# Linear attention with decay feeding a routed expert layer: attention with transposed output, alternating halves of the matmul array and interleaved sequences

## The chip, the cores and the metric

The kernel runs on one core of one Trainium2 chip. The metric is the device time of one execution in microseconds. The engines named below are TensorE (PE for its matmuls, PEld for its weight loads), VectorE (DVE), ScalarE (ACT), GpSimd (POOL) and the queue of SyncE (SP), which here only issues transfers.

## What is computed

There are 4 sequences of 768 tokens and 8 heads of 64. Attention is linear with a decay per head, and each token's result (512 numbers) then goes through one of 8 experts.

```python
# attention, per head, with lam the decay
intra = (q_b @ k_b.T) * Dmask @ v_b          # Dmask[i, j] = lam ** (i - j) where i >= j
inter = (q_b * lam_pow) @ kv_state
out_b = intra + inter
kv_state = lam_block * kv_state + (k_b * rev_pow).T @ v_b
# expert layer, x = attention's output as (B, S, 512)
logits = x @ w_gate                           # 8 experts
local_gate = sigmoid(x @ w_local)
e = argmax(logits) if s == 0 or local_gate < 0.5 else previous token's e
out = softmax(logits)[e] * (relu(x @ w1[e]) @ w2[e])
```

All inputs and matmuls are float32.

## The kernel before

There are three stages. **Attention** (function `attention(b)`, L135 to L207) goes through the sequences one after the other and through each in 6 chunks of 128 positions (the reference's blocks of 64 give the same result with chunks of any size). **Routing** (L213 to L347) finds each token's expert and sorts tokens into 31 tiles of 128 slots. **Experts** (L349 to L409) gather each tile's rows from DRAM, run the two matrices of its expert and scatter the result.

Attention loads three chunks at a time, with four transfers on SP's queue (`qt`, `kt`: q and k with the head dimension on the partitions, two heads in the two halves of the 128 partitions; `kn`, `vn`: k and v with positions on the partitions). The experts' first weights (four transfers of 2 MB, L150 and L151) follow the loads of the second half of sequence 0. Then, for each chunk:

- the scores (L168), 8 matmuls: keys as the stationary operand, queries moving, each on 64 rows of the array (one head); the half `u` = 0 first, then `u` = 1. VectorE multiplies each half by the decay mask into `sm` (L170);
- the output `po` (L174, L178): the decayed queries `qd` times the state `kv` (4 matmuls, two heads at once), and for each of 8 heads `sm` as the stationary operand of 128 columns, `v` moving with 64 columns. The positions are on the partitions of the result;
- the state (L184 to L194): 4 matmuls into `pk`; GpSimd scales the old state (L190), VectorE adds `pk` (L192), in two halves;
- the way out: ScalarE copies `po` to `xn` (L196) and issues its transfer to `x_dram` (L197); TensorE transposes `xn` (L200, 4 transposes); ScalarE copies them to `xt` (L202); 4 matmuls with `xt` stationary and the gate's 9 columns moving give the logits in `pl` (L204), which VectorE copies to `lt` once per three chunks (L207).

GpSimd also makes `qd` (L153, three chunks at once) and `kd`, the decayed keys (L156, one per chunk). The order of the instructions on each engine is that of a scheduler, which fills TensorE's waits of one chunk with work of the next. Matmuls in float32 appear in the trace as two records each.

Of the kernel before, what the change touches and what calls it, by code (L numbers as in the profile page):

```python
# [8 lines left out]
F32 = mybir.dt.float32  # L9
I32 = mybir.dt.int32  # L10
U32 = mybir.dt.uint32
# [3 lines left out]
SP = mybir.EngineType.SP  # L15
PSUM = bass.MemoryType.PSUM
# [11 lines left out]
HC = 3                  # chunks per load  # L28
# [9 lines left out]
def kernel(  # L38
    ctx: ExitStack,
    tc: tile.TileContext,  # L40
    qT: bass.AP,
    kT: bass.AP,
    k: bass.AP,
    v: bass.AP,
# [26 lines left out]
    lamb = const.tile([P, H], F32, name="lamb")  # L71
    nc.sync.dma_start(out=lamb, in_=lam.unsqueeze(0).broadcast_to([P, H]))
    wgt = const.tile([P, DT, E + 1], F32, name="wgt")
    nc.sync.dma_start(out=wgt, in_=wg)
# [19 lines left out]
    token = iota("token", [[P, NT]], 1, 1)      # the token's row, plus one  # L94
    whole = iota("whole", [[P, NT]], 0, 0)      # 0, 128, 256, ...

    x_ctx = ExitStack()
    load = x_ctx.enter_context(tc.tile_pool(name="load", bufs=2))
# [4 lines left out]
    # mask[j, u, a, i] = lam[2a + u] ** (i - j) where i >= j, else 0  # L103
# [4 lines left out]
    with tc.tile_pool(name="build", bufs=1) as build:  # L108
# [9 lines left out]
        # lamq[(u d), a, i] = lam[2a + u] ** (i + 1)  # L118
# [16 lines left out]
    def attention(b):  # L135
        kv = att.tile([P, A, 2, DH], F32, name="kv")
        nc.gpsimd.memset(kv, 0.0)
        for half in range(NC // HC):
            r = slice(HC * P * half, HC * P * half + HC * P)
            qt = load.tile([P, A, HC, P], F32, name="qt")  # L140
            nc.sync.dma_start(out=qt.rearrange("p a c i -> p a (c i)"), in_=qT[b, :, :, r])
            kt = load.tile([P, A, HC, P], F32, name="kt")
            nc.sync.dma_start(out=kt.rearrange("p a c i -> p a (c i)"), in_=kT[b, :, :, r])
            kn = load.tile([P, HC, DM], F32, name="kn")
            nc.sync.dma_start(out=kn, in_=k[b, r].rearrange("(c p) d -> p c d", p=P))
            vn = load.tile([P, HC, DM], F32, name="vn")
            nc.sync.dma_start(out=vn, in_=v[b, r].rearrange("(c p) d -> p c d", p=P))
            if b == 0 and half == 1:
                for i in range(2):
                    nc.sync.dma_start(out=w1t[i], in_=w1_src(0))  # L150
                    nc.sync.dma_start(out=w2t[i], in_=w2_src(0))  # L151
            qd = att.tile([P, A, HC, P], F32, name="qd")
            nc.gpsimd.tensor_tensor(qd, qt, lamq.unsqueeze(2).broadcast_to([P, A, HC, P]), ALU.mult)  # L153
            kd = att.tile([P, HC, DM], F32, name="kd")
            for c in range(HC):
                nc.gpsimd.tensor_tensor(kd[:, c].rearrange("p (h d) -> p h d", d=DH),  # L156
                                        kn[:, c].rearrange("p (h d) -> p h d", d=DH),
                                        rev.unsqueeze(2).broadcast_to([P, H, DH]), ALU.mult)
            pl = pa.tile([P, HC, E + 1], F32, name="pl")
            for c in range(HC):  # L160
                ch = HC * half + c
                t = NC * b + ch
                sm = att.tile([P, 2, A, P], F32, name="sm")
                for u in range(2):
                    rows = slice(DH * u, DH * u + DH)
                    ps = pa.tile([P, A, P], F32, name="ps", bufs=2)
# [3 lines left out]
                    nc.vector.tensor_tensor(sm[:, u], ps, mask[:, u], ALU.mult)  # L170
                po = pa.tile([P, A, 2, DH], F32, name="po", bufs=2)
                for a in range(A):
                    if ch:
                        nc.tensor.matmul(po[:, a], lhsT=qd[:, a, c], rhs=kv[:, a],  # L174
                                         start=True, stop=False, skip_group_check=True)
                    for u in range(2):
# [3 lines left out]
                if ch + 1 < NC:  # L180
                    pk = pa.tile([P, A, 2, DH], F32, name="pk")
                    for a in range(A):
                        cols = slice(P * a, P * a + P)
                        nc.tensor.matmul(pk[:, a], lhsT=kd[:, c, cols], rhs=vn[:, c, cols],  # L184
                                         start=True, stop=True)
                    for u in range(2):
                        rows = slice(DH * u, DH * u + DH)
                        d = kv[rows, :, u]
                        if ch:
                            nc.gpsimd.tensor_tensor(d, d, lamq[rows, :, P - 1:P].broadcast_to([DH, A, DH]),  # L190
                                                    ALU.mult)
                            nc.vector.tensor_tensor(d, pk[rows, :, u], d, ALU.add)  # L192
                        else:
                            nc.vector.tensor_copy(d, pk[rows, :, u])  # L194
                xn = att.tile([P, DM], F32, name="xn", bufs=3)
                nc.scalar.copy(xn, po.rearrange("p a u d -> p (a u d)"))  # L196
                nc.scalar.dma_start(out=x_dram[P * t:P * t + P, :], in_=xn)  # L197
                pt = pa.tile([P, DT, P], F32, name="pt")
                for d in range(DT):
                    nc.tensor.transpose(pt[:, d], xn[:, P * d:P * d + P], ident)  # L200
                xt = att.tile([P, DT, P], F32, name="xt")
                nc.scalar.copy(xt, pt)  # L202
                for d in range(DT):
                    nc.tensor.matmul(pl[:, c], lhsT=xt[:, d], rhs=wgt[:, d],  # L204
                                     start=(d == 0), stop=(d == DT - 1))
            t = NC * b + HC * half
            nc.vector.tensor_copy(lt[:, t:t + HC], pl)  # L207

    for b in range(B):
        attention(b)  # L210
    x_ctx.close()

# [1 line left out]
    gidx = route.tile([P, G], U32, name="gidx")     # row of x for each slot  # L214
    sidx = route.tile([P, G], U32, name="sidx")     # row of out for each slot
    gate = route.tile([P, G], F32, name="gate")
    owner = route.tile([1, G], I32, name="owner")   # each tile's expert
    with tc.tile_pool(name="rt", bufs=1) as rt, tc.tile_pool(name="pr", bufs=1, space=PSUM) as pr:
# [4 lines left out]
        # the first of the greatest, as 8 - e  # L223
# [33 lines left out]
        # is[p, e, t]: token (t, p) goes to expert e  # L257
# [4 lines left out]
        # the chosen expert's probability  # L262
# [83 lines left out]
        nc.vector.tensor_tensor(src, src, none, ALU.add)  # L346
        nc.vector.tensor_copy(sidx, src)  # L347

# [97 lines left out]
```

## Time and profile before

| | us |
|---|---|
| two runs | 720.13 and 730.7, median 725.41 |
| span of the profiled execution | 743.7 |
| attention: first scores to the last copy into `lt` | 8.9 to 248.6 |
| experts: first expert matmul to the end | 287.4 to 743.7 |

TensorE is busy 702.7 us of the span (94%), VectorE 128.5 (17%), ScalarE 66.8 (9%), GpSimd 136.3 (18%). The page is one profiled execution. Its second part cuts the span in 40 slices of 18.6 us; PEclk is the clock that TensorE was granted, in tenths of full speed (9 and more is 2.4 GHz throughout, 5 is 1.2 GHz). A timeline row merges neighbouring instructions of the same line and says when the first began, how long they lasted and how many there were.

### The profile page before, as it was taken

What the parts mean: (1) busy time and instruction counts of PE and PEld (TensorE: products, weight loads), DVE (VectorE), ACT (ScalarE), POOL (GpSimd) and SP (SyncE); (2) the same over time, 40 slices, a digit from 0 to 9 for tenths busy, and PEclk for the clock granted to TensorE, in tenths of its full rate; (3) what the DMA queues carried; (4) which work ended last, traced back from release to release, by engine and by line L of the source; (5) the groups of instructions that cost most, each with busy time, mean ns of one, the idle gap of its engine ahead of it and who ended that gap; (6) DMA issues with size and microseconds to landing.
All of it is one profiled execution on the core that took longest, in us unless ns stands there. A gap on an engine that the chain in (4) does not pass through costs nothing. (4 is left out here: it accounts for less than half of the span.)

```text
span 743.7 us, 9546 instructions
## 1 busy us (share of the span) xinstructions
PE 702.7 (94%) x4056; PEld 560.5 (75%) x4056; DVE 128.5 (17%) x250; ACT 66.8 (9%) x112; POOL 136.3 (18%) x140
## 2 busy tenths in 40 slices
PE   4999999999999566999999999999999999999995
PEld 4998998989998456677677767767776776777673
DVE  6221221111113471010110101011010101101010
ACT  0110111000001000001000000100000010000000
POOL 6315532042101002111111111111111111111010
PEclk9995985555579657999999999999999999999999
DMA  8996543220401002049294771680583838610000
GB/s 304 402 332 235 175 174 120 70 100 15 152 18 43 15 1 71 29 165 341 88 328 154 266 257 41 235 281 29 207 308 129 309 127 312 208 43 25 1 1 0
DMA packets 48683, 113.63 MB, mean 153 GB/s; under 512 B 3134, under 2 KB 11326, under 8 KB 48640
## 3 DMA queue, kind: packets, MB, share of 16 engines
q1 hardware_dynamic: 40224, 92.30, 35.5%
q0 software_dynamic: 4960, 14.43, 5.6%
q10 hardware_dynamic: 3456, 6.29, 2.2%
q8 instruction: 32, 0.52, 0.3%
q14 instruction: 11, 0.09, 0.0%
HBM read 171.73 MB, written 14.42 MB: 250 GB/s over the span
## 5 line engine op out<-in xcount | busy, mean ns | idle before, releaser
L383 PEld LDWEIGHTS ph<-xtm,w 128*128 128x128 f32 x1984 | 227.6, 193 | 14.3 <-issue 14.3
L383 PE MATMUL ph<-xtm,w 128*128 128x128 f32 x1984 | 227.7, 276 | 0.0
L391 PE MATMUL py<-w,ht 128*128 128x512 f32 x496 | 218.0, 593 | 0.0
L391 PEld LDWEIGHTS py<-w,ht 128*128 128x128 f32 x496 | 92.0, 191 | 103.6 <-issue 103.6
L168 PE MATMUL ps<-qt,kt 64*128 64x128 f32 x384 | 72.7, 378 | 10.4 <-DMA kt<-in_kT_dram 8.9
L385 ACT ACTIVATE ht<-ph 128x512 f32<-128x512 f32 x62 | 37.0, 597 | 442.4 <-PE ph L383 442.4
L394 POOL DMA_INDIRECT out_dram<-y,sidx x31 | 31.4, 1013 | 242.3 <-DVE y L393 242.3
L178 PE MATMUL po<-vn,sm 128*128 128x64 f32 x384 | 74.2, 328 | 0.4 <-DVE sm L170 0.4
L178 PEld LDWEIGHTS po<-vn,sm 128*128 128x128 f32 x384 | 71.5, 259 | 2.0 <-issue 1.3
L168 PEld LDWEIGHTS ps<-qt,kt 64*128 64x128 f32 x384 | 57.5, 256 | 19.5 <-issue 15.4
L364 POOL DMA_INDIRECT xg<-x_dram,gidx x31 | 30.2, 976 | 194.8 <-PE ptm L371 144.6
L393 DVE TENSOR_SCALAR y<-py,gate 128x512 f32<-128x512 f32 x31 | 23.3, 751 | 206.8 <-PE py L391 206.8
L373 DVE COPY xtm<-ptm 128x512 f32<-128x512 f32 x31 | 21.5, 692 | 204.5 <-PE ptm L371 204.5
L174 PE MATMUL po<-kv,qd 128*128 128x128 f32 x160 | 45.6, 375 | 0.0
L170 DVE TENSOR_TENSOR sm<-ps,mask 128x512 f32<-128x512 f32 x48 | 33.1, 691 | 71.2 <-PE ps L168 71.1
L190 POOL TENSOR_TENSOR kv<-kv,lamq 64x256 f32<-64x256 f32 x32 | 19.7, 616 | 132.5 <-PE po L174 131.3
L184 PE MATMUL pk<-vn,kd 128*128 128x128 f32 x160 | 35.2, 358 | 0.0
L204 PEld LDWEIGHTS pl<-wgt,xt 128*128 128x128 f32 x192 | 30.7, 243 | 4.9 <-ACT xt L202 2.2
L174 PEld LDWEIGHTS po<-kv,qd 128*128 128x128 f32 x160 | 31.4, 244 | 3.2 <-issue 1.8
L204 PE MATMUL pl<-wgt,xt 128*128 128x9 f32 x192 | 32.2, 296 | 1.4 <-ACT xt L202 1.3
L153 POOL TENSOR_TENSOR qd<-qt,lamq 128x1536 f32<-128x1536 f32 x8 | 27.6, 3446 | 14.4 <-PE po L174 9.9
L196 ACT COPY xn<-po 128x512 f32<-128x512 f32 x24 | 14.0, 585 | 176.1 <-PE po L178 176.1
(101 smaller groups left out, 229.0 us busy)
## 6 DMA issues: line engine op xcount, KB each, us to landing
w<-in_w_dram SPq DMA_DIRECT2D x66, 2048.0 KB
qt<-in_qT_dram SPq DMA_DIRECT2D x8, 768.0 KB
kt<-in_kT_dram SPq DMA_DIRECT2D x8, 768.0 KB
kn<-in_k_dram SPq DMA_DIRECT2D x8, 768.0 KB
vn<-in_v_dram SPq DMA_DIRECT2D x8, 768.0 KB
x_dram<-xn ACTq DMA_DIRECT2D x24, 256.0 KB
xg<-x_dram,gidx POOLq DMA_INDIRECT x31, 4.3
out_dram<-y,sidx POOLq DMA_INDIRECT x31, 4.0
```

Of the source, the lines that this page charges most:

```text
L153: nc.gpsimd.tensor_tensor(qd, qt, lamq.unsqueeze(2).broadcast_to([P, A, HC, P]), ALU.mult)
L168: nc.tensor.matmul(ps[:, a], lhsT=kt[rows, a, c], rhs=qt[rows, a, c], start=True, stop=True)
L170: nc.vector.tensor_tensor(sm[:, u], ps, mask[:, u], ALU.mult)
L174: nc.tensor.matmul(po[:, a], lhsT=qd[:, a, c], rhs=kv[:, a], start=True, stop=False, skip_group_check=True)
L178: nc.tensor.matmul(po[:, a, u], lhsT=sm[:, u, a], rhs=vn[:, c, DH * h:DH * h + DH], start=not ch, stop=True, skip_group_check=True)
L184: nc.tensor.matmul(pk[:, a], lhsT=kd[:, c, cols], rhs=vn[:, c, cols], start=True, stop=True)
L204: nc.tensor.matmul(pl[:, c], lhsT=xt[:, d], rhs=wgt[:, d], start=(d == 0), stop=(d == DT - 1))
L364: nc.gpsimd.indirect_dma_start(out=xg, out_offset=None, in_=x_dram[:, :], in_offset=bass.IndirectOffsetOnAxis(ap=gidx[:, g:g + 1], axis=0))
L383: nc.tensor.matmul(ph[:, i], lhsT=w1t[g % 2][:, d, P * f:P * f + P], rhs=xt[:, d], start=(d == 0), stop=(d == DT - 1))
L385: nc.scalar.activation(ht[:, FT // 2 * half:FT // 2 * half + FT // 2], ph, ACT.Relu)
L391: nc.tensor.matmul(py, lhsT=ht[:, f], rhs=w2t[g % 2][:, f], start=(f == 0), stop=(f == FT - 1))
L394: nc.gpsimd.indirect_dma_start(out=out, out_offset=bass.IndirectOffsetOnAxis(ap=sidx[:, g:g + 1], axis=0), in_=y, in_offset=None, bounds_c ...
```

## The change

Attention is rewritten; routing and experts are the same text. The sequences are interleaved: step `s` is chunk `c` of sequence `b` in the order (0,0), (1,0), (2,0), (3,0), (0,1) and so on, 24 steps, with a state for each sequence. q, k (transposed) and k, v (natural) of a chunk are packed into one array by the host and come in one transfer of 1 MB with six buffers. The scores alternate between the two row halves. `v` is now the stationary operand (64 columns) and `sm` moves (128 columns), so the result `po` is already transposed; the two heads go to the two column halves of the array. ScalarE copies `po` to `xt` first; TensorE then transposes `xt` into `pt`, which becomes `xn` for DRAM. For the logits the gate, padded to 32 columns, is stationary and `xt` moves; the four parts of the sum over 512 go to four column quarters, ScalarE copies them to `lg`, and a matmul with `fold` as moving operand adds the four parts and transposes them. VectorE copies that to `lt` once per step. TensorE's order is written by hand: in step `s` it does the scores of `s+1`, the output and state of `s`, the fold of `s-2`, and the transposes and logits of `s-1`. The weights of the first expert are loaded in four pieces at steps 8, 12, 16 and 20.

```diff
...
-                    for a in range(A):
-                        nc.tensor.matmul(ps[:, a], lhsT=kt[rows, a, c], rhs=qt[rows, a, c],
-                                         start=True, stop=True)
...
-                    for u in range(2):
-                        h = 2 * a + u
-                        nc.tensor.matmul(po[:, a, u], lhsT=sm[:, u, a], rhs=vn[:, c, DH * h:DH * h + DH],
-                                         start=not ch, stop=True, skip_group_check=True)
...
-                for d in range(DT):
-                    nc.tensor.matmul(pl[:, c], lhsT=xt[:, d], rhs=wgt[:, d],
-                                     start=(d == 0), stop=(d == DT - 1))
...
+    load = x_ctx.enter_context(tc.tile_pool(name="load", bufs=6))
...
+    def fetch(s):
+        b, c = ORDER[s]
+        x = inp[s] = load.tile([P, 4, DM], F32, name="inp")
+        nc.sync.dma_start(out=x, in_=qkv[s])
+        if c:
+            qd = qds[s] = att.tile([P, A, P], F32, name="qd", bufs=3)
+            nc.gpsimd.tensor_tensor(qd, x[:, 0].rearrange("p (a i) -> p a i", i=P), lamq, ALU.mult)
+        if c + 1 < NC:
+            kd = kds[s] = att.tile([P, DM], F32, name="kd", bufs=3)
+            nc.gpsimd.tensor_tensor(kd.rearrange("p (h d) -> p h d", d=DH),
+                                    x[:, 2].rearrange("p (h d) -> p h d", d=DH),
+                                    rev.unsqueeze(2).broadcast_to([P, H, DH]), ALU.mult)
+
+    def scores(s):
...
+        ps = [pa.tile([P, A, P], F32, name=f"ps{u}", bufs=2) for u in range(2)]
+        for a in range(A):
+            for u in range(2):
+                rows = slice(DH * u, DH * u + DH)
+                nc.tensor.matmul(ps[u][:, a], lhsT=kt[rows, a], rhs=qt[rows, a], start=True, stop=True)
+        sm = sms[s] = att.tile([P, 2, A, P], F32, name="sm")
+        for u in range(2):
+            nc.vector.tensor_tensor(sm[:, u], ps[u], mask[:, u], ALU.mult)
+
+    def mix(s):
...
+        po = pa.tile([P, A, P], F32, name="po")
+        if c:
+            qd = qds.pop(s)
+            for a in range(A):
+                nc.tensor.matmul(po[:, a], lhsT=kv[:, a].rearrange("p u d -> p (u d)"), rhs=qd[:, a],
+                                 start=(a == 0), stop=False, skip_group_check=True)
+        for a in range(A):
+            for u in range(2):
+                nc.tensor.matmul(po[DH * u:DH * u + DH, a], lhsT=vn[:, a, u], rhs=sm[:, u, a],
+                                 start=(not c and a == 0), stop=(a == A - 1), skip_group_check=True)
+        xt = xts[s] = att.tile([P, A, P], F32, name="xt")
+        nc.scalar.copy(xt, po)
+        if c + 1 < NC:
...
+                nc.tensor.matmul(pk[:, a], lhsT=kd[:, cols], rhs=x[:, 3, cols], start=True, stop=True)
...
+                if c:
+                    nc.gpsimd.tensor_tensor(d, d, lamq[rows, :, P - 1:P].broadcast_to([DH, A, DH]), ALU.mult)
+                    nc.vector.tensor_tensor(d, pk[rows, :, u], d, ALU.add)
...
+    def leave(s):
...
+        for d in range(DT):
+            nc.tensor.transpose(pt[:, P * d:P * d + P], xt[:, d], ident)
+        xn = att.tile([P, DM], F32, name="xn")
+        nc.scalar.copy(xn, pt)
...
+        pl = pls[s] = pa.tile([P, P + E + 1], F32, name="pl")
+        for d in range(DT):
+            nc.tensor.matmul(pl[EP * d:EP * d + EP, :P], lhsT=wgt[:, d], rhs=xt[:, d], start=True, stop=True,
+                             skip_group_check=True)
+        lg = lgs[s] = att.tile([P, P], F32, name="lg")
+        nc.scalar.copy(lg, pl[:, :P])
+
+    def logits(s):
...
+        nc.tensor.matmul(pl[:, P:], lhsT=lgs.pop(s), rhs=fold, start=True, stop=True, skip_group_check=True)
+        nc.vector.tensor_copy(lt[:, NC * b + c], pl[:, P:])
...
+            if s + 1 < NS:
+                scores(s + 1)
+            if s < NS:
+                mix(s)
+            if 0 <= s - 2 < NS:
+                logits(s - 2)
+            if 0 <= s - 1 < NS:
+                leave(s - 1)
```

The tiles `po`, `pk`, `pt` and `pl` have one buffer each, `ps0` and `ps1` two each.

On TensorE, before, a chunk in the middle of a sequence (the last part of one chunk's output, then the next chunk's scores, which the scheduler has put among the transposes and logits):

```order
L178 MATMUL po<-vn,sm 128x64
L174 MATMUL po<-kv,qd 128x128
L178 MATMUL po<-vn,sm 128x64 x2
L174 MATMUL po<-kv,qd 128x128
L178 MATMUL po<-vn,sm 128x64 x2
L174 MATMUL po<-kv,qd 128x128
L178 MATMUL po<-vn,sm 128x64 x2
L184 MATMUL pk<-vn,kd 128x128
L168 MATMUL ps<-qt,kt 128x128 x3
L200 MATMUL pt<-ident,xn 128x128 x4
L168 MATMUL ps<-qt,kt 128x128 x4
L204 MATMUL pl<-wgt,xt 128x9 x4
```

On TensorE now, one step in the middle, from the state's part of the output to the beginning of the next scores (L184 state times `qd`, L188 `v` times `sm`, L197 state update, L227 fold, L212 transposes, L219 logits, L171 scores; the pair of L171 rows comes four times in a row):

```order
L184 MATMUL po<-qd,kv_138 128x128 x4
L188 MATMUL po<-sm,inp 64x128 x8
L197 MATMUL pk<-inp,kd 128x128 x4
L227 MATMUL pl<-fold,lg 128x9
L212 MATMUL pt<-ident,xt 128x128 x4
L219 MATMUL pl<-xt,wgt 32x128 x4
L171 MATMUL ps_675<-inp 128x128
L171 MATMUL ps_676<-inp 128x128
```

What moved: each kind of matmul now stands in one block per step, the two score tiles take turns, and no score stands between the transposes and the logits.

On VectorE now, the same place (L174 the masks, L203 the two halves of the state, L228 the logits of two steps earlier):

```order
L203 TENSOR_TENSOR kv_144<-pk,kv_144 64x4x64 x2
L228 COPY lt<-pl 128x9
L174 TENSOR_TENSOR sm<-ps_615,mask 128x512
L174 TENSOR_TENSOR sm<-ps_616,mask 128x512
L203 TENSOR_TENSOR kv_138<-pk,kv_138 64x4x64 x2
L228 COPY lt<-pl 128x9
```

What moved: before, the copy into `lt` came once per three chunks; now one comes in every step, and it stands behind the two halves of the state.

On GpSimd, before, the work for three chunks of a sequence (L153 `qd` for three chunks, L190 the scaling of the state, L156 `kd`):

```order
L153 TENSOR_TENSOR qd<-qt,lamq 128x1536
L190 TENSOR_TENSOR kv<-kv,lamq 64x4x64 x4
L156 TENSOR_TENSOR kd<-kn,rev 128x512 x3
L153 TENSOR_TENSOR qd<-qt,lamq 128x1536
L190 TENSOR_TENSOR kv<-kv,lamq 64x4x64 x4
```

And now (L156 `qd`, L202 the scaling, L159 `kd`):

```order
L156 TENSOR_TENSOR qd<-inp,lamq 128x512
L202 TENSOR_TENSOR kv_138<-kv_138,lamq 64x4x64 x2
L159 TENSOR_TENSOR kd<-inp,rev 128x512
L156 TENSOR_TENSOR qd<-inp,lamq 128x512
L202 TENSOR_TENSOR kv_140<-kv_140,lamq 64x4x64 x2
```

What moved: `qd` for the step three ahead now stands in front of every scaling of a state, and it writes into one of three buffers that the state's matmuls of the current step read last.

## Rows read from the trace of the kernel before

**Rows 1.** The page: its heading, and the granted clock in 40 slices

```profile
span 743.7 us, 9546 instructions
...
PEclk9995985555579657999999999999999999999999
```

**Rows 2.** Stretches: length, busy PE, PEld, DVE, ACT, POOL (count), clock, DMA share, GB/s

```profile
15.00:50.00 35.00, 35.00 (x262) 32.44 (x261) 9.34 (x18) 5.27 (x9) 11.96 (x13) 1.00 1.04 394
...
106.00:213.00 107.00, 107.00 (x464) 97.03 (x463) 17.20 (x32) 9.36 (x16) 21.78 (x18) 0.50 0.28 94
215.00:245.00 30.00, 29.81 (x240) 26.98 (x238) 9.10 (x17) 4.68 (x8) 4.93 (x8) 1.00 0.09 36
```

**Rows 3.** Timeline, end of attention: start us, us, engine, line, operation, tiles, count

```profile
244.71 0.56 PE L178 MATMUL po<-vn,sm 128*128 128x64 f32 x4
...
248.37 0.19 DVE L207 COPY lt<-pl 128x27 f32<-128x27 f32 x1 [2.55 <-PE pl L204]
```

**Rows 4.** Timeline of TensorE's matmuls, one chunk at full clock

```profile
79.72 0.49 PE L168 MATMUL ps<-qt,kt 64*128 64x128 f32 x2
80.14 0.66 PE L200 MATMUL pt<-ident,xn 128*128 128x128 f32 x4
80.73 0.72 PE L168 MATMUL ps<-qt,kt 64*128 64x128 f32 x8
81.47 1.06 PE L204 MATMUL pl<-wgt,xt 128*128 128x9 f32 x8
82.46 0.71 PE L168 MATMUL ps<-qt,kt 64*128 64x128 f32 x4
83.10 0.49 PE L174 MATMUL po<-kv,qd 128*128 128x128 f32 x2
...
89.19 1.06 PE L204 MATMUL pl<-wgt,xt 128*128 128x9 f32 x8
```

**Rows 5.** Timeline of TensorE's matmuls, one chunk at half clock

```profile
127.47 1.87 PE L204 MATMUL pl<-wgt,xt 128*128 128x9 f32 x8
129.27 0.79 PE L168 MATMUL ps<-qt,kt 64*128 64x128 f32 x2
129.99 0.79 PE L174 MATMUL po<-kv,qd 128*128 128x128 f32 x2
...
141.32 1.88 PE L204 MATMUL pl<-wgt,xt 128*128 128x9 f32 x8
```

**Rows 6.** Timeline, the start of attention

```profile
6.97 3.86 DVE L90 CAST token<-token_i 128x24 f32<-128x24 int32 x1
...
12.68 0.17 DVE L132 COPY rev<-mask 128x8 f32<-128x8 f32 x1
...
15.66 3.67 PE L178 MATMUL po<-vn,sm 128*128 128x64 f32 x16
```

**Rows 7.** Timeline of GpSimd and VectorE, one chunk at full clock

```profile
86.35 1.31 POOL L190 TENSOR_TENSOR kv<-kv,lamq 64x256 f32<-64x256 f32 x2 [3.16 <-PE po L174]
...
87.69 0.43 DVE L192 TENSOR_TENSOR kv<-pk,kv 64x256 f32<-64x256 f32 x1 [0.23 <-POOL kv L190]
...
87.74 3.04 POOL L156 TENSOR_TENSOR kd<-kn,rev 128x512 f32<-128x512 f32 x3
...
88.84 0.69 DVE L170 TENSOR_TENSOR sm<-ps,mask 128x512 f32<-128x512 f32 x1 [0.72 <-PE ps L168]
...
90.28 0.19 DVE L207 COPY lt<-pl 128x27 f32<-128x27 f32 x1 [0.75 <-PE pl L204]
...
90.74 3.45 POOL L153 TENSOR_TENSOR qd<-qt,lamq 128x1536 f32<-128x1536 f32 x1
```

**Rows 8.** TensorE's timeline, before a rise (74.3 us) and a fall (105.3)

```profile
71.45 2.02 PE L184 MATMUL pk<-vn,kd 128*128 128x128 f32 x8
...
102.71 0.66 PE L200 MATMUL pt<-ident,xn 128*128 128x128 f32 x4
...
104.16 1.06 PE L204 MATMUL pl<-wgt,xt 128*128 128x9 f32 x8
```

More of the change, by code (lines that the diff above doesn't have):

```diff
@@ L15 @@
 SP = mybir.EngineType.SP
+PE = mybir.EngineType.PE
 PSUM = bass.MemoryType.PSUM
@@ L27 @@
 NC = S // P
-HC = 3
+ORDER = [(b, c) for c in range(NC) for b in range(B)]
+EP = 32
 G = (N + E * (P - 1)) // P
@@ L72 @@
     nc.sync.dma_start(out=lamb, in_=lam.unsqueeze(0).broadcast_to([P, H]))
-    wgt = const.tile([P, DT, E + 1], F32, name="wgt")
-    nc.sync.dma_start(out=wgt, in_=wg)
+    wgt = const.tile([P, DT, EP], F32, name="wgt")
+    nc.gpsimd.memset(wgt, 0.0)
+    nc.sync.dma_start(out=wgt[:, :, :E + 1], in_=wg)
     ident = const.tile([P, P], F32, name="ident")
@@ L95 @@
     whole = iota("whole", [[P, NT]], 0, 0)
+    fold = const.tile([P, E + 1], F32, name="fold")
+    nc.vector.tensor_tensor(fold, ident[:, 0:E + 1], ident[:, EP:EP + E + 1], ALU.add)
+    for d in range(2, DT):
+        nc.vector.tensor_tensor(fold, fold, ident[:, EP * d:EP * d + E + 1], ALU.add)
     x_ctx = ExitStack()
-    load = x_ctx.enter_context(tc.tile_pool(name="load", bufs=2))
+    load = x_ctx.enter_context(tc.tile_pool(name="load", bufs=6))
     att = x_ctx.enter_context(tc.tile_pool(name="att", bufs=2))
@@ L132 @@
     nc.vector.tensor_copy(rev.rearrange("p (a u) -> p u a", u=2), mask[:, :, :, P - 1])
-    def attention(b):
-        kv = att.tile([P, A, 2, DH], F32, name="kv")
+    NS = len(ORDER)
+    kvs = []
+    for b in range(B):
+        kv = pows.tile([P, A, 2, DH], F32, name=f"kv{b}")
         nc.gpsimd.memset(kv, 0.0)
[L138 to L163, printed above, removed]
-                for u in range(2):
-                    rows = slice(DH * u, DH * u + DH)
-                    ps = pa.tile([P, A, P], F32, name="ps", bufs=2)
-                    for a in range(A):
-                        nc.tensor.matmul(ps[:, a], lhsT=kt[rows, a, c], rhs=qt[rows, a, c],
-                                         start=True, stop=True)
[L170 to L176, printed above, removed]
-                        h = 2 * a + u
-                        nc.tensor.matmul(po[:, a, u], lhsT=sm[:, u, a], rhs=vn[:, c, DH * h:DH * h + DH],
-                                         start=not ch, stop=True, skip_group_check=True)
[L180 to L198, printed above, removed]
-                for d in range(DT):
[L200 to L203, printed above, removed]
-                    nc.tensor.matmul(pl[:, c], lhsT=xt[:, d], rhs=wgt[:, d],
-                                     start=(d == 0), stop=(d == DT - 1))
-            t = NC * b + HC * half
-            nc.vector.tensor_copy(lt[:, t:t + HC], pl)
@@ L209 @@
-    for b in range(B):
-        attention(b)
+        kvs.append(kv)
+    inp, qds, kds, sms, xts, lgs = {}, {}, {}, {}, {}, {}
+    def fetch(s):
[10 more added lines that the diff above has]
+                                    rev.unsqueeze(2).broadcast_to([P, H, DH]), ALU.mult)
@@ new lines, in mix @@
+    def mix(s):
+        b, c = ORDER[s]
+        kv, sm, x = kvs[b], sms.pop(s), inp.pop(s)
+        vn = x[:, 3].rearrange("p (a u d) -> p a u d", u=2, d=DH)
+        po = pa.tile([P, A, P], F32, name="po")
[11 more added lines that the diff above has]
+        if c + 1 < NC:
+            kd = kds.pop(s)
+            pk = pa.tile([P, A, 2, DH], F32, name="pk")
+            for a in range(A):
+                cols = slice(P * a, P * a + P)
+                nc.tensor.matmul(pk[:, a], lhsT=kd[:, cols], rhs=x[:, 3, cols], start=True, stop=True)
+            for u in range(2):
+                rows = slice(DH * u, DH * u + DH)
+                d = kv[rows, :, u]
+                if c:
+                    nc.gpsimd.tensor_tensor(d, d, lamq[rows, :, P - 1:P].broadcast_to([DH, A, DH]), ALU.mult)
+                    nc.vector.tensor_tensor(d, pk[rows, :, u], d, ALU.add)
+                else:
+                    nc.vector.tensor_copy(d, pk[rows, :, u])
@@ new lines, in logits @@
+    def logits(s):
+        b, c = ORDER[s]
+        pl = pls.pop(s)
+        nc.tensor.matmul(pl[:, P:], lhsT=lgs.pop(s), rhs=fold, start=True, stop=True, skip_group_check=True)
+        nc.vector.tensor_copy(lt[:, NC * b + c], pl[:, P:])
+    pls = {}
+    with tc.manual_schedule(engines={PE}):
+        for s in range(3):
+            fetch(s)
+        scores(0)
+        for s in range(NS + 2):
+            if s + 3 < NS:
+                fetch(s + 3)
+            if s in (8, 12, 16, 20):
+                i, second = divmod(s // 4 - 2, 2)
+                nc.sync.dma_start(out=(w2t if second else w1t)[i], in_=(w2_src if second else w1_src)(0))
+            if s + 1 < NS:
[6 more added lines that the diff above has]
+                leave(s - 1)
@@ L421, in turned @@
     def turned(a):
[L422 removed]
+        return a.reshape(B, A, 2, NC, P, DH).transpose(0, 3, 2, 5, 1, 4).reshape(B, NC, P, DM)
     def natural(a):
[L425 removed]
+        return a.transpose(0, 2, 1, 3).reshape(B, NC, P, DM)
+    packed = _np.stack([turned(i["q"]), turned(i["k"]), natural(i["k"]), natural(i["v"])], 3)
     arrays = {
[L428 to L431 removed]
+        "qkv": _np.stack([packed[b, c] for b, c in ORDER]),
         "lam": i["lam"],
```

19 lines of the change are left out of this document (9 added, 10 removed).

## The prediction

> **What bounds the kernel now.** I read the stages first. The page gives TensorE 94% busy of a 743.7 us span, at full clock in some slices and half in others [rows 1]. The busy share per stretch says that attention, from 9 to 248 us, keeps the matmul engine full, and that the time depends on the granted clock: at 1.00 thirty us hold 240 matmul records, at 0.50 a hundred and seven hold 464, so a record takes 0.125 or 0.23 us [rows 2]. VectorE, ScalarE and GpSimd are busy less than a third of those stretches. The experts, from about 290 on, run at full clock [rows 1] and are not edited; routing between them only waits on VectorE and is not edited. So the change can act only on what lies before the last copy into `lt`, which ends at 248.4 + 0.2 = 248.6 us [rows 3].
>
> Next, TensorE's own order of time inside one chunk [rows 4]. Each matmul in float32 leaves two records, a transpose one. The starts give the price: two score records at 79.72 let the transposes start at 80.14 (0.42 us), four at 82.46 let L174 start at 83.10 (0.64). So a record costs 0.11 and leaving a stretch of 64-row matmuls 0.20 more. The 9-column logits at 81.47 cost as much as others: eight records and the step out of them take 0.99 until 82.46, because each loads 128 columns of weights. From one logits group to the next, a chunk, it is 81.47 to 89.19, 7.7 us. At half clock two score records take 0.72 (129.27 to 129.99) and a chunk 13.9 (127.47 to 141.32) [rows 5]; sixteen records at 15.66 last 3.67 [rows 6]. So at half clock a record is 0.21 and the change of shape 0.30. By that row the first 23 us were at half clock too, whatever the page's clock row says there.
>
> The row on which most rests is the one at 80.73: eight score records in 0.72 us, where four at 82.46 take 0.71 [rows 4]. There the end of one row half (two matmuls) and the beginning of the other (two) were issued next to each other, and they ran side by side.
>
> **The change, part by part.** Per chunk ("step") TensorE now does, in a written order: scores of s+1, state x q, v x scores, the state update, one fold, four transposes, logits.
>
> *Scores:* still 16 records, now alternating row halves throughout: 8 pairs x 0.11 + 0.20 = 1.08. If only one half ran at a time, 1.96.
>
> *v x scores (L178 before):* still 16 records with 128 columns moving instead of 64, alternating column halves. No row of before has column halves. Bounds: one after the other, 16 x 0.11 + 0.20 = 1.96; side by side as the row halves at 80.73, 1.08. I take 1.08, the nearest row. The Trainium skill, "TensorEngine Tiling (Array Packing)", Key Properties, says the same of tiles in general, that they load and multiply independently; no row here shows it for columns.
>
> *Logits:* before 8 records; now 8 with 32 weight columns in four column quarters plus a fold of 2. Side by side 2 x 0.11 + 0.20 = 0.42, in turn 1.08; fold 0.22. I take 0.42.
>
> *State x q, state update, transposes:* unchanged in number: 0.88 + 0.20, 0.88, 0.44 + 0.20.
>
> *Changes of shape:* the sum holds five per step, into and out of row halves, column halves, column quarters, at 0.20 each. The rows show the 0.20 only for 64-row stretches; that column shapes pay it is my reading. The same section of the skill speaks here against the change: changing the tiling mode drains the array. Rows agree for row tiling, with 0.20 us. Without that price for the three column changes a step would be 0.6 us shorter, by the rule it is as summed.
>
> Sum for a full step: 1.08 + 1.08 + 1.08 + 0.88 + 0.22 + 0.64 + 0.42 = 5.40 us.
>
> *A new wait.* `pl` has one buffer: the logits of s-1 may start only when VectorE has copied the fold of s-2, and VectorE's queue has the two state additions of s ahead of that copy. These wait for GpSimd, which after state x q of step s first makes `qd` of s+3 and then scales the state. From the end of state x q: 3.45/3 = 1.15 (qd), 1.31 (two scalings), 0.43 (the second addition), 0.19 (the copy) [rows 7], plus four hand-overs of about 0.04 (87.66 to 87.69 in that view): 3.25 us. TensorE itself arrives after 0.11 + 0.20 + 1.08 + 0.88 + 0.22 + 0.64, less the 0.28 by which a last record outlasts its start (0.49 - 0.21 at 83.10): 2.85. So it waits 0.40, and a full step takes 5.80. Behind the waiting logits on TensorE stand the next scores and the next state x q, and for these GpSimd waits: a ring of 5.80 us.
>
> *Hidden:* ScalarE now makes two copies of 0.58 (4.68 us for 8 [rows 2]) and a small one; GpSimd 1.15 + 1.01 + 1.31 = 3.5 of 5.8 us [rows 7]; VectorE 2 x 0.69 + 0.86 + 0.19 = 2.4. The inputs come as 1.05 MB per chunk, six buffers, so a load has about five steps to land. All bytes up to the end of attention (25.2 MB in, 8.4 MB weights, 6.3 MB out) need 101 us at the 394 GB/s that before reached while the engines were full [rows 2]; attention below takes more. Cost nothing; if the rate halved, about 55 us.
>
> *Start.* Before, `rev` came at 12.7 us because a small cast at 6.97 took 3.86 us while GpSimd worked, and the first v x scores began at 15.66 [rows 6]. Now GpSimd has no `qd` to make for four steps, so the mask and `rev` should be ready near 10, and mix(0) starts near 11.7. Steps 0 and 1 at half clock: 1.98 + 1.7 and 1.98 + 1.98 + 1.7 + 1.14 + 0.72, to about 23, where before also came to full clock. Steps 2 and 3 have no state x q: 4.32 each, to 31.6. Steps 4 to 19: 16 x 5.80, to 124.4. Steps 20 to 23 have no state update and no scaling: 3 x 4.52 + 3.44, to 141.4. A tail of 3.3 as before (last v x scores out at 245.3, `lt` at 248.6 [rows 3]): 144.7.
>
> So attention ends 248.6 - 144.7 = 104 us earlier, and 743.7 - 104 = 640. This is on the scale of the profiled execution, 743.7; the median of the runs shown is 725.4. I carry no offset over: a chunk at half clock costs 6.2 us more, so three fewer such chunks explain 18 us, and in the changed kernel I expect hardly any. Were the gap the profile's own, the time would be 622.
>
> **The clock.** Before, it fell after a stretch of half-row scores, transposes and 9-column logits [rows 8], and rose right after the state update at 71.45 and the transposes behind it [rows 8]. The change removes the 9-column stretch and packs the scores, so I forecast that it stays at full clock once there.
>
> **Rivals.**
> - *Column halves run in turn.* The row for row halves at 80.73 is all that speaks against it. v x scores +0.88, logits +0.66 a step; the 0.40 wait disappears: 6.94 for steps 4 to 19 (+18), +1.54 in the six other full-clock steps (+9), +5 in the two slow ones: 672.
> - *The ring is longer than priced* (GpSimd slower beside VectorE, a hand-over more). One to three us a step for 16 steps: 656 to 688.
> - *The clock stays at half.* A step is then 40 units of 0.21 and five changes of 0.30, 9.9; attention ends near 233: 728, no change. Against it: the 9-column stretch before the fall is gone [rows 8]. For it: there are more changes of shape with idle array.
> - *Slower: each alternation of halves costs like a change of shape.* A matmul of two records in either kind of half then takes 0.42: scores and v x scores 3.36 each, logits 1.68, a step 11.2, attention over 260, and the time about 765. It decides from 0.2 us per alternation (20 a step, 24 steps, 100 us). The row at 80.73 speaks against it for row halves; for column halves alone it would be about 718.
>
> **How the numbers follow.** Forecast 0.64 (its own range 615 to 656), column halves in turn 0.20, a longer ring 0.08, half clock 0.05, alternation 0.03. Low 615 is 640 less the 18 of the profile's offset and 7 for full clock from the first steps; high 690 takes in the second and third case. Two per cent, about what a measurement of this kernel can tell, is 711 and 740: faster 0.92, within 0.05 (half clock), slower 0.03.
>
> **What would show it.** In the changed kernel's trace: L171 records starting two at a time, 16 of them in about 1 us; the same for L188, or else 16 starts 0.11 apart (the first rival); L219 idle about 0.4 us behind VectorE's copy; a step of 5.8 us from one L212 group to the next; granted clock 1.00 from about 23 us; `lt` complete near 145 us. I am wrong if the step is over 7 us, or if loads become what the scores wait for.

## The result, and the profile after

The changed kernel takes **639.42 us** (two runs, 638.1 and 640.74) against 725.41 before: a ratio of 0.8814, with a 95% interval of 0.8527 to 0.9102. The forecast was 640.0, within 615 to 690. The interval is that wide because of the kernel before: over all its runs here it takes 720 to 754 us, with a mean granted clock of 0.917 at 719.87 and 0.872 at 753.52, while the changed kernel keeps to 638 to 642. The ratios below leave the slowest runs of the kernel before out, so they are not the quotients of the medians.

The page of the profiled execution (640.74 us, of which the span is 639.0), heading and granted clock in 40 slices of 16 us; compare [rows 1]:

```profile
span 639.0 us, 9717 instructions
...
PEclk9999999995579999999999999999999999999998
```

The three low slices are routing, after attention. Inside attention the clock no longer falls. The stretches (length, then busy time and count of PE, PEld, DVE, ACT and POOL, granted clock, DMA share, GB/s) say the same:

```profile
15.00:144.00 129.00, 116.37 (x1373) 96.98 (x1372) 49.80 (x112) 33.45 (x72) 62.23 (x69) 1.00 0.74 273
144.00:184.00 40.00, 20.89 (x91) 18.45 (x92) 23.34 (x75) 0.36 (x1) 4.82 (x5) 0.50 0.10 29
```

Attention now ends at 144, fully clocked from 15 on, but TensorE stands still for 12.6 of the 129 us, where it was full, or nearly, before [rows 2]. The timeline shows where: the start, one step in the middle, and the last copy into `lt` (start us, us, engine, line, operation, tiles, shapes, count, and in brackets the idle time ahead of it with what ended it). Rows that the text does not need are left out between these.

```profile
7.48 0.17 DVE L90 CAST token<-token_i 128x24 f32<-128x24 int32 x1
10.04 0.17 DVE L138 COPY rev<-mask 128x8 f32<-128x8 f32 x1
10.48 2.08 PE L171 MATMUL ps<-inp 64*128 64x128 f32 x16 [0.93 <-DMA inp<-in_qkv_dram]
12.49 1.97 PE L188 MATMUL po<-sm,inp 128*64 128x128 f32 x16
16.58 1.09 PE L188 MATMUL po<-sm,inp 128*64 128x128 f32 x16
22.86 0.87 DVE L205 COPY kv<-pk 64x256 f32<-64x256 f32 x2 [0.90 <-PE pk L197]
23.77 0.17 DVE L228 COPY lt<-pl 128x9 f32<-128x9 f32 x1
23.99 0.43 PE L219 MATMUL pl<-xt,wgt 128*32 128x128 f32 x8 [0.62 <-DVE lt L228]
...
70.58 0.42 PE L219 MATMUL pl<-xt,wgt 128*32 128x128 f32 x8 [0.62 <-DVE lt L228]
70.93 1.16 PE L171 MATMUL ps<-inp 64*128 64x128 f32 x16
72.02 1.16 PE L184 MATMUL po<-qd,kv 128*128 128x128 f32 x8
73.11 1.09 PE L188 MATMUL po<-sm,inp 128*64 128x128 f32 x16
73.26 1.27 POOL L156 TENSOR_TENSOR qd<-inp,lamq 128x512 f32<-128x512 f32 x1 [2.29 <-PE po L184]
74.14 1.16 PE L197 MATMUL pk<-inp,kd 128*128 128x128 f32 x8
74.50 1.31 POOL L202 TENSOR_TENSOR kv<-kv,lamq 64x256 f32<-64x256 f32 x2
75.13 0.29 PE L227 MATMUL pl<-fold,lg 128*128 128x9 f32 x2
75.27 0.63 PE L212 MATMUL pt<-ident,xt 128*128 128x128 f32 x4
75.40 0.88 DVE L203 TENSOR_TENSOR kv<-pk,kv 64x256 f32<-64x256 f32 x2 [1.99 <-PE pk L197]
76.31 0.17 DVE L228 COPY lt<-pl 128x9 f32<-128x9 f32 x1
76.53 0.43 PE L219 MATMUL pl<-xt,wgt 128*32 128x128 f32 x8 [0.62 <-DVE lt L228]
...
143.70 0.17 DVE L228 COPY lt<-pl 128x9 f32<-128x9 f32 x1 [1.55 <-PE pl L227]
```

The last copy ends at 143.87, where it ended at 248.56 before [rows 3]: 104.7 us. Behind it the time is the same: 743.7 - 248.6 and 639.0 - 143.9 both leave 495.1 us.

The stillness has one name in the waits (engine, tile and line that waited, for whom; us in total, times, longest):

```profile
PE pl L219 <- DVE lt L228: 11.3, 18, 0.7
```

### The profile page after: what moved, and what is told of

It is laid out like the page before. It is cut to its first block, busy times and chain, and to the rows that moved or that the text cites. A ratio compares the mean times of both kernels' runs of the same rounds, so it can differ in the third digit from the quotient of the medians.

```text
span 639.0 us, 9717 instructions
## 1 busy us (share of the span) xinstructions
PE 590.9 (92%) x4104; PEld 449.3 (70%) x4104; DVE 126.3 (20%) x269; ACT 72.6 (11%) x136; POOL 130.4 (20%) x149
## 5 line engine op out<-in xcount | busy, mean ns | idle before, releaser
L421 PEld LDWEIGHTS ph<-xtm,w 128*128 128x128 f32 x1984 | 227.5, 193 | 14.4 <-issue 14.4
L174 DVE TENSOR_TENSOR sm<-ps,mask 128x512 f32<-128x512 f32 x48 | 30.9, 686 | 34.6 <-PE ps L171 34.5
L171 PE MATMUL ps<-inp 64*128 64x128 f32 x384 | 29.7, 297 | 8.4 <-DMA inp<-in_qkv_dram 8.4
L156 POOL TENSOR_TENSOR qd<-inp,lamq 128x512 f32<-128x512 f32 x20 | 25.5, 1274 | 44.6 <-PE po L184 29.8
L171 PEld LDWEIGHTS ps<-inp 64*128 64x128 f32 x384 | 24.9, 199 | 13.0 <-DMA inp<-in_qkv_dram 8.7
L188 PE MATMUL po<-sm,inp 128*64 128x128 f32 x384 | 27.1, 285 | 0.0
L409 PE MATMUL ptm<-ident,xg 128*128 128x128 f32 x124 | 19.6, 283 | 6.0 <-DMA xg<-x_dram,gidx 6.0
L159 POOL TENSOR_TENSOR kd<-inp,rev 128x512 f32<-128x512 f32 x20 | 20.8, 1043 | 13.2 <-DVE rev L138 6.3
L188 PEld LDWEIGHTS po<-sm,inp 128*64 128x64 f32 x384 | 21.2, 140 | 3.0 <-issue 0.2
L184 PE MATMUL po<-qd,kv 128*128 128x128 f32 x160 | 23.2, 288 | 0.0
L197 PE MATMUL pk<-inp,kd 128*128 128x128 f32 x160 | 23.2, 288 | 0.0
L197 PEld LDWEIGHTS pk<-inp,kd 128*128 128x128 f32 x160 | 19.4, 191 | 3.6 <-issue 3.3
L184 PEld LDWEIGHTS po<-qd,kv 128*128 128x128 f32 x160 | 19.4, 191 | 2.5 <-issue 0.2
```

The lines of the kernel that those rows point to most:

```text
L156: nc.gpsimd.tensor_tensor(qd, x[:, 0].rearrange("p (a i) -> p a i", i=P), lamq, ALU.mult)
L171: nc.tensor.matmul(ps[u][:, a], lhsT=kt[rows, a], rhs=qt[rows, a], start=True, stop=True)
L174: nc.vector.tensor_tensor(sm[:, u], ps[u], mask[:, u], ALU.mult)
L184: nc.tensor.matmul(po[:, a], lhsT=kv[:, a].rearrange("p u d -> p (u d)"), rhs=qd[:, a], start=(a == 0), stop=False, skip_group_check=True)
L188: nc.tensor.matmul(po[DH * u:DH * u + DH, a], lhsT=vn[:, a, u], rhs=sm[:, u, a], start=(not c and a == 0), stop=(a == A - 1), skip_group_c ...
L197: nc.tensor.matmul(pk[:, a], lhsT=kd[:, cols], rhs=x[:, 3, cols], start=True, stop=True)
```

## The experiments

Each kernel below was timed in several rounds beside the kernel before. The first four ran on one chip (the kernel before there: 736.78 to 753.52), the last four on another (719.87 to 753.6). The version with the fold ahead, from which the last four start, was not run again on the second chip.

| kernel | median us | lowest to highest | last `lt` copy ends, us |
|---|---|---|---|
| changed kernel, unedited | 640.84 | 640.13 to 641.77 | 144.4 |
| fold ahead of the output | 629.28 | 628.35 to 629.8 | 132.4 |
| output not turned | 653.62 | 652.86 to 657.0 | 157.0 |
| before, gate of 128 columns | 689.8 | 688.57 to 689.99 | 192.6 |
| fold ahead, row halves in turn | 642.86 | 641.16 to 644.56 | 147.2 |
| fold ahead, column halves in turn | 640.55 | 640.14 to 642.43 | 145.2 |
| fold ahead, sequences one by one | 630.51 | 628.06 to 630.79 | 133.4 |
| fold ahead, four loads per chunk | 630.07 | 629.4 to 630.86 | 132.5 |

In all of them 495 to 496 us of the span lie behind the last copy, so a time and the end of attention say nearly the same thing.

### The changed kernel again

No edit; it is what the next two are compared with.

> The changed kernel again, on the chip of the next three, as their measure. 638 to 641 us, a step of 5.96 us from one group of logits matmuls to the next, full clock through attention from about 15 us on.

Measured: 640.84, ratio 0.8651 (0.8544 to 0.8757). Its profiled execution took 641.77 us with a span of 640.0, so 1.8 us lie around the span.

### The fold ahead of the output

The suspected ring is: `pl` has one buffer, its copy stands in VectorE's queue behind the two state additions, these wait for GpSimd's scaling, and that for `qd`. The edit issues the fold and its copy before the output and state of the same step; the arithmetic is the same.

```diff
+            if 0 <= s - 2 < NS:
+                logits(s - 2)
             if s < NS:
                 mix(s)
-            if 0 <= s - 2 < NS:
-                logits(s - 2)
```

> The changed kernel with one edit: on TensorE the fold of s-2 comes ahead of the output of s instead of behind its state update, so that VectorE copies it before the two additions of s. My theory: the logits of s-1 then no longer wait for the ring over GpSimd and VectorE (0.62 us idle per step in the changed kernel), the step falls from 5.96 to about 5.4 us, the time to 628 to 631. Rival: the wait only moves to another place of the same ring (the state update waits for its buffer, or state times q for qd): step 5.9, time 637 to 640.

Measured: 629.28, ratio to before 0.8494 (0.8389 to 0.8598); 11.6 us less than the changed kernel. Its timeline, one step, without rows that the text does not need:

```profile
70.14 1.16 PE L171 MATMUL ps<-inp 64*128 64x128 f32 x16
71.23 0.39 PE L227 MATMUL pl<-fold,lg 128*128 128x9 f32 x2
71.48 1.14 PE L184 MATMUL po<-qd,kv 128*128 128x128 f32 x8
72.54 0.16 DVE L228 COPY lt<-pl 128x9 f32<-128x9 f32 x1
72.55 1.09 PE L188 MATMUL po<-sm,inp 128*64 128x128 f32 x16
73.93 1.31 POOL L202 TENSOR_TENSOR kv<-kv,lamq 64x256 f32<-64x256 f32 x2
74.83 0.88 DVE L203 TENSOR_TENSOR kv<-pk,kv 64x256 f32<-64x256 f32 x2 [2.14 <-PE pk L197]
75.09 0.42 PE L219 MATMUL pl<-xt,wgt 128*32 128x128 f32 x8
75.45 1.16 PE L171 MATMUL ps<-inp 64*128 64x128 f32 x16
```

and its stretch from 25 to 125 us:

```profile
25.00:125.00 100.00, 100.00 (x1180) 85.02 (x1177) 41.16 (x94) 25.55 (x58) 55.34 (x64) 1.00 0.83 305
```

The copy at 72.54 now stands ahead of the additions at 74.83, and the logits at 75.09 find `pl` free: no bracket. A step is 75.45 - 70.14 = 5.31 us and TensorE is busy 100.00 of 100 us. The 11.3 us of the waits above account for the 11.6 us of the times. So the wait for VectorE's copy was a real cost of the change, and one that two moved lines remove; this version beats both kernels. It shows that the copy's place behind the additions was the cause. That GpSimd held the additions up it does not show, and the trace of the changed kernel speaks against it (see the wait, below).

### The output not turned

The changed kernel with `po` back in its old form: `sm` stationary with 128 columns, `v` moving with 64, transposes of `xn`, and logits with 9 moving columns that need no fold. The written order, alternating row halves, interleaving and packed loads stay, but for two things that follow from the old form: state x q and v x scores take turns again, and the logits of step s-2 stand where the fold stood.

```diff
-                nc.tensor.matmul(po[DH * u:DH * u + DH, a], lhsT=vn[:, a, u], rhs=sm[:, u, a],
+                nc.tensor.matmul(po[:, a, u], lhsT=sm[:, u, a], rhs=vn[:, a, u],
...
-            nc.tensor.matmul(pl[EP * d:EP * d + EP, :P], lhsT=wgt[:, d], rhs=xt[:, d], start=True, stop=True,
+            nc.tensor.matmul(pl, lhsT=xt[:, d], rhs=wgt[:, d, :E + 1], start=(d == 0), stop=(d == DT - 1))
```

> The changed kernel with the turned output taken back: sm stationary and v moving with 64 columns, positions on the partitions, then transposes, then 9-column logits with xt stationary and no fold; order by hand, alternating row halves, interleaving and packed loads stay. Theory A, the turned output itself gains little: TensorE has 52 record slots of 0.11 and two changes of shape of 0.20 per step, 6.1 us against 5.96, and the clock stays full: 640 to 648 us. Theory B, the turned output carries the gain: either the step grows by the 0.88 and 0.66 us that column halves and quarters save (7.0 us or more, 660 or more), or the clock falls to half again in some stretch because of 64- and 9-column matmuls (680 or more).

Measured: 653.62, 12.8 us above the changed kernel. One step and the stretch from 25 to 125:

```profile
70.43 1.16 PE L171 MATMUL ps<-inp 64*128 64x128 f32 x16
...
75.20 0.96 PE L222 MATMUL pl<-wgt,xt 128*128 128x9 f32 x8
76.01 0.63 PE L213 MATMUL pt<-ident,xn 128*128 128x128 f32 x4
76.58 1.16 PE L171 MATMUL ps<-inp 64*128 64x128 f32 x16
```

```profile
25.00:125.00 100.00, 100.00 (x978) 95.37 (x977) 37.37 (x81) 19.34 (x33) 53.17 (x61) 1.00 0.83 304
```

The expectation (640 to 648) fell short by some 6 us because it went by the step alone. A step is 6.15 us with no wait in it, where the changed kernel needs 5.95 with 0.62 of waiting; over 16 steps that is only 3 us of the 13. Another 4 lie in the start: without turned output the first v x scores takes 3.47 us instead of 1.91, records are at full pitch only from 20.2 us, and the fifth scores begin at 28.33 instead of 24.35. When the pitch rises is not fixed by the kernel alone: in the second profile of the changed kernel the fifth scores begin at 24.84. The other 6 are in the last steps, where the changed kernel has no wait and needs 4.37 each, against 5.25 here. So the turned output was worth 13 us as it stands. Against the version with the fold ahead it is worth 24: the wait had eaten nearly half of it. The clock stayed full, with moving operands of 9 and 64 columns in every step; this matters below.

### The kernel before with a gate of 128 columns

How much of the gain is the clock alone? Before, the clock fell after stretches that contain the 9-column logits [rows 8]. This edit pads the gate with zeros, so that the logits move 128 columns. Every count in attention stays; the scheduler's order on TensorE differs in three places, where one matmul of the state update and one of the scores stand later. The first of these places is at 76 us in the kernel before, behind the first fall of its clock [rows 1], so the order does not explain that fall.

```diff
-    wgt = const.tile([P, DT, E + 1], F32, name="wgt")
-    nc.sync.dma_start(out=wgt, in_=wg)
+    wgt = const.tile([P, DT, P], F32, name="wgt")
+    nc.gpsimd.memset(wgt, 0.0)
+    nc.sync.dma_start(out=wgt[:, :, :E + 1], in_=wg)
```

> The kernel before with one edit: the gate is padded with zeros to 128 columns, so that the logits matmuls move 128 columns instead of 9 (their weight load of 128 columns is the same, so a record should still take 0.11 us). More work, nothing saved. Theory: what stood before the falls of the clock (half-row scores, transposes, 9-column logits) was the cause; with full columns the clock no longer falls in attention, a chunk stays at 7.6 us, attention ends near 195 us and the time is 670 to 695. Rival: the falls have another cause (waits, row halves, chance): granted clock 0.5 over some 100 us as before, 715 to 745.

Measured: 689.8, ratio 0.9309 (0.9195 to 0.9424). Its granted clock, its logits, and its last copy:

```profile
PEclk9999999999955699999999999999999999999999
```

```profile
109.42 1.16 PE L205 MATMUL pl<-wgt,xt 128*128 128x128 f32 x8
110.51 0.71 PE L169 MATMUL ps<-qt,kt 64*128 64x128 f32 x4
...
192.36 0.19 DVE L208 COPY lt<-pl 128x27 f32<-128x27 f32 x1 [3.49 <-PE pl L205]
```

The logits cost 1.09 us instead of the 0.99 at 81.47 [rows 4], about 2 us over 24 chunks, and the clock then stays full from 23 us to the end of attention. More work, and 7% less time. The mean granted clock is 0.966 to 0.968 in all four runs, where the kernel before has 0.872 to 0.917 in all 14 that were timed beside these kernels. This splits the 104.7 us of the two profiles: 248.6 to 192.6 is the clock (56 us), 192.6 to 157.0 is the written order with its alternating halves, interleaving and loads (36), and 157.0 to 143.9 the turned output (13). The first of the three is that of one execution: against the runs of the kernel before, 720 to 754 us, it is 30 to 64 us, and 36 against the median of 725.41.

### Halves in turn

Two kernels with the fold ahead, in which only the order of two loops is swapped: in one for the scores, in the other for v x scores. All matmuls of one half then stand ahead of those of the other.

```diff
-        for a in range(A):
-            for u in range(2):
+        for u in range(2):
+            for a in range(A):
```

> The kernel with the fold moved ahead (629.3 us, a step of 5.31 us in which TensorE never idles), with one edit: the scores in the order of before, all four matmuls of one row half, then all four of the other. Theory: issuing the halves alternately is what brings them together; in the kernel before, at its first scores, the second half began only when three records of the first were left to start, so 16 records took the place of 12 or 13. Then a step grows by 0.4 to 0.5 us and the time to 639 to 641. Rival 1: the matmul queue looks far enough ahead by itself: no change, 628 to 631. Rival 2: nothing overlaps: +0.88 per step, 649 to 652.

> The same base (629.3 us), with the matmuls of v with the scores issued for all of one column half, then all of the other, instead of alternately. Theory: column halves behave as row halves, with the same short look ahead: a step grows by 0.4 to 0.5 us, 639 to 641. Rival 1: no change, 628 to 631. Rival 2: +0.88, 649 to 652.

Measured: 642.86 with row halves in turn (13.6 above the version with the fold ahead, and above the 639 to 641 expected) and 640.55 with column halves in turn (11.3 above). Beside the next two kernels, which ran on the same chip and differ little from the version with the fold ahead, it is 12.4 to 12.8 and 10.0 to 10.5 us. The timelines, row halves first:

```profile
72.99 1.71 PE L171 MATMUL ps<-inp 64*128 64x128 f32 x16
74.63 0.39 PE L227 MATMUL pl<-fold,lg 128*128 128x9 f32 x2
```

```profile
73.71 1.58 PE L188 MATMUL po<-sm,inp 128*64 128x128 f32 x16
75.22 1.16 PE L197 MATMUL pk<-inp,kd 128*128 128x128 f32 x8
```

The scores take 1.64 us to the next shape instead of 1.09, v x scores 1.51 instead of 1.02; 24 times 0.55 and 0.49 are 13.2 and 11.8 us, near the two differences. It is not the 1.96 of halves that run one after the other: the single records show the second half of the scores beginning 0.55 us after the first, once five records of that have started, so about three pairs still overlap. For columns the second half begins 0.49 us after the first, again once five records have started. The overlap depends on the order of issue, for columns as for rows.

### Interleaving and the packed load

On the version with the fold ahead, first the sequences one after the other, then four transfers of 256 KB per chunk instead of one of 1 MB.

```diff
-ORDER = [(b, c) for c in range(NC) for b in range(B)]
+ORDER = [(b, c) for b in range(B) for c in range(NC)]
```

```diff
-        nc.sync.dma_start(out=x, in_=qkv[s])
+        for i in range(4):
+            nc.sync.dma_start(out=x[:, i], in_=qkv[s][:, i])
```

> The same base (629.3 us), with the sequences one after the other as before instead of interleaved; nothing else. Theory: interleaving buys nothing at this pace, since the new state of a chunk is ready about 1 us before the next chunk's state times q (additions end at 75.7, those matmuls begin at 76.8 in the base): 628 to 632 us. Rival: with the same state in every step, scaling, additions and the next matmuls form a ring that is longer than 5.31 us: 640 or more.

> The same base (629.3 us), with each chunk's 1 MB fetched in four transfers of 256 KB (2 KB per partition) instead of one. Theory: loads are hidden behind five steps of lead either way: 628 to 631 us. Rival: four times as many issues on SyncE and smaller pieces slow the loads until the scores wait for them: 635 or more.

Measured: 630.51 and 630.07 against 629.28, all three with overlapping runs. The step is the same 5.31 us in each. The first scores start at 6.57 instead of 7.45 us with four loads, and nothing comes of it at the end. Neither part of the change moves the time by an amount that these runs can tell.

## Why the prediction was right

**The frame held.** Only what lies before the last copy into `lt` changed, and the 495.1 us behind it are the same. To carry no offset over was right too: about 2 us lie around the span, and the 18 us between the profile of before and its median are within that kernel's own spread, so that the gain is 105 us between the two profiles and 86 between the medians.

**The sum of a step**, each term from one start to the next, the transposes to the end of their last record, where the wait begins:

| term | predicted us | measured us |
|---|---|---|
| scores | 1.08 | 1.09 |
| state x q | 1.08 | 1.09 |
| v x scores | 1.08 | 1.03 |
| state update | 0.88 | 0.99 |
| fold | 0.22 | 0.14 |
| transposes | 0.64 | 0.64 |
| wait for `lt` | 0.40 | 0.62 |
| logits | 0.42 | 0.35 |
| step | 5.80 | 5.95 |

*Column halves* were the term with the widest bounds, 1.08 to 1.96, and the first rival (0.20) stood on it. The nearest row, that of the row halves at 80.73 [rows 4], gave the right end, and it was a choice by analogy: L188 takes 1.03 us for 16 records. The logits in four column quarters take 0.35. The rival's order can be had by swapping two loops, and even then it costs 0.49 us a step and not 0.88. The Trainium skill, "TensorEngine Tiling (Array Packing)", Key Properties, has tiles load and multiply independently. The trace agrees for columns, with the 1.03 us. The order of issue decides too, as the two kernels with halves in turn show.

*Changes of shape.* The price of 0.20, put on column shapes by analogy, is there, a little smaller. Over what their records need at 0.11 a pair or a record, scores take 0.21 more, state x q 0.21, v x scores 0.15 and the logits in column quarters 0.13. The state update takes 0.11 more, where nothing had been put, and the fold behind it 0.08 less. What the transposes pay is hidden by the wait; with the fold ahead they take 0.53 us to the next start, 0.09 more than their records need. The Trainium skill, in the same section, has a change of mode drain the array. The trace agrees for columns too, with the 0.15 and 0.13 us. The rival in which each alternation of halves costs like a change of shape is refuted: 16 alternating records take 1.09 and 1.03 us.

*The wait* was rightly put on VectorE's copy behind the two additions, and the fold ahead shows it by removing it. What the additions wait for was read wrongly. The prediction followed only the path over GpSimd, which makes `qd`, scales the state and so releases the second addition. It left out that the additions also need `pk`, the result of the state update on TensorE itself. VectorE's waits, and the single instructions of the step shown above (the second scaling, the second addition), tell which came last:

```profile
DVE kv L203 <- PE pk L197: 31.8, 16, 2.0
```

```profile
75.18 0.62 POOL L202 TENSOR_TENSOR kv<-kv,lamq 64x256 f32<-64x256 f32 x1
75.85 0.43 DVE L203 TENSOR_TENSOR kv<-pk,kv 64x256 f32<-64x256 f32 x1
```

In all 16 steps with a scaling it is `pk` that releases the first addition, here at 75.40, 0.10 after the state update ends (74.14 + 1.16 = 75.30). The second follows at 75.85, behind the first (75.40 + 0.42 = 75.82) and behind the scaling (75.80) alike. Steps 2 and 3 scale nothing: there two plain copies of `pk` stand ahead of the copy into `lt`, as at 22.86, and TensorE waits the same 0.62. So the wait needs no GpSimd; its scaling ends just in time, and only in three of the 16 steps after the first addition, by up to 0.04 us.

The size was short for the same reason. From the end of state x q (72.02 + 1.16 = 73.18) the copy lets the logits start at 76.53, after 3.35 us, predicted 3.25. By the prediction's own prices the path over `pk` is longer than the one it took: 0.20 + 1.08 + 0.88 to the end of `pk`, 0.86 for the additions, 0.19 for the copy and four hand-overs of 0.04 are an estimated 3.37 us. TensorE would have been ready at 75.27 + 0.64 = 75.91, after 2.73, predicted 2.85, because v x scores, the fold and the way out of state x q were shorter by more than the state update was longer. The two small misses make the wait 0.62 instead of 0.40. The rival of a ring longer by 1 to 3 us did not come.

**The start was mis-sized.** `rev` came at 10.04 as said (12.68 before [rows 6]), and the small cast took 0.17 us instead of 3.86, with GpSimd idle beside it. But the first v x scores began only at 12.49, not at 11.7, because the scores of step 1 ahead of them waited 0.93 us for their load (10.48); without that they would have begun at 11.56. Full pitch came at 14.4 us and not at 23: the 16 records at 12.49 take 1.91 us up to the next line, those at 16.58 take 1.02. So step 2 began (scores of step 3) at 19.48 instead of 23.0, 3.5 us less. Against it, steps 2 and 3 wait for `lt` as well, at 4.87 us instead of 4.32 (1.1 us), and the 16 full steps cost 0.16 more each (2.6 us); what follows them is 1.0 us shorter. So 143.9 against 144.7 is closer than its parts by luck: two errors of about 3.5 us with opposite signs cancelled. The term that failed is that of steps 0 and 1, which put both at half clock as the first 23 us of the kernel before were.

**The clock** stayed full, as forecast. It was also the largest part of the gain between the two profiles, 56 of 105 us (between the medians 36 of 86), which the sum holds without naming it. The reason given, that the 9-column stretch goes and the scores are packed, is borne out in one half: widening those 9 columns alone keeps the clock of the kernel before full. But with the written order 9-column logits do no harm (output not turned, full clock throughout). What in the old order makes those columns matter is open. No run takes the scheduler's order with 9 columns and only the halves changed.

**Loads** were costed at nothing, and past the 0.93 us in the start they cost nothing. With the fold ahead the DMA share is 0.83 from 25 to 125 us and TensorE is nevertheless full; four transfers in place of one change no time.

Not separated: how the 36 us between the padded kernel before and the kernel without turned output divide among the written order, the alternating halves for all scores, and fewer changes of shape. Row halves in turn alone cost 12.4 to 13.6 us in the kernel with the fold ahead; that is one part of it, and some 3 us are scores that begin earlier (7.37 us instead of 10.53).

## What to carry to other kernels

Read the price of a pair of matmuls and of a change of shape off one chunk of the kernel before, and the step of a rewritten order can be summed from them to a few per cent (here 5.80 against 5.95 us); interleave the matmuls that go to different parts of the array, since issued in turn they overlap only in part. Where a tile has one buffer, follow its release through the in-order queue of the engine that frees it: here a 0.17 us copy stood behind two additions that waited for the state update of the same step, and issuing it earlier gave 11.6 us. Price every input of the instructions ahead of it: the path that was left out was the one that ended last. Where TensorE is full and its clock is half, the shapes in the stretch ahead of the fall are worth one padded run before anything is rewritten.

## What the runs showed of the hardware that was not expected

- **The granted clock falls under a full TensorE.** In the kernel before it was at 0.50 for 107 us in which the engine was busy 107.00 of them [rows 2]. Padding a moving operand from 9 to 128 columns with zeros removed the fall and saved 7% of the time. The Trainium skill, "TensorE: Matmul & The Clock Gate", HAM oscillation, ties a fall of the clock to gaps in which TensorE stands idle. This trace differs: in the kernel before, the stretch ahead of the fall at 105.3 is full, 10.30 of 10.30 us.

```profile
95.00:105.30 10.30, 10.30 (x84) 9.20 (x83) 3.55 (x7) 1.76 (x3) 4.26 (x6) 1.00 0.25 94
```

- **Narrow moving operands do not by themselves bring the clock down.** With 9-column logits and 64-column v in a written order it stayed at 1.00 from 25 to 125 us.
- **Halves issued one after the other overlap only in part.** With one half's eight records ahead of the other's, the second starts 0.55 us (rows) or 0.49 us (columns) late, and 16 records take 1.64 us (rows) or 1.51 us (columns) instead of 1.09 or 1.02.
